# Keeping GpSimd's indirect transfers apart in a pooled-attention and top-1 mixture-of-experts kernel

## The chip, the cores and the metric

The kernel runs on one core of one Trainium2 chip. The metric is device time in microseconds (us) for one execution, the median of several runs; lower is better. The core's engines are named as in the profile: PE (TensorE, matmul), PEld (its weight loads), DVE (VectorE), ACT (ScalarE), POOL (GpSimd) and SP (SyncE, which here only issues DMAs).

## The reference

q, k and v are of shape 8 x 8 x 1152 x 64 (batch, heads, sequence, head size). Queries are averaged in pairs, attention is taken over the 576 pooled queries, and its output, one row of 512 per pooled query, goes through a mixture of 8 experts of which each token uses the one with the largest logit:

```python
q_pool = q.reshape(B, H, S // 2, 2, D).mean(axis=3)
attn = softmax(q_pool @ k.T / sqrt(D)); x = (attn @ v) as 4608 rows of 512
expert_idx = argmax(x @ w_gate); gate_w = softmax(x @ w_gate) at expert_idx
for e in range(8):                      # w1[e]: 512 x 1024, w2[e]: 1024 x 512
    out[mask_e] = gate_w[mask_e] * (relu(x[mask_e] @ w1[e]) @ w2[e])
```

## The kernel before, in words

**Attention** goes over 8 batches, 4 pairs of heads each, two halves of the queries per pair. PE makes the scores (`scores`, L521: 9 steps of 8 matmul records per half), DVE scales them and takes the minimum (L525), a small matmul and a reduce make one bias for the half (L543, L549), ACT takes the exponent (L553), POOL folds the chunks for the sums (L599) and PE multiplies with v (`values`, L624). For the last three pairs of the last batch PE makes the sums from the unfolded chunks (L594), and POOL has no folds.

**Routing** (`routing`) follows each batch: logits, the expert of each token, its place in that expert's list. ACT, DVE and SP write the batch's rows to a DRAM buffer `x_runs` (`put`), and POOL writes token numbers and weights into the experts' lists with six indirect scatters of 96 entries (`enlist`, L799). For batches 0 to 5 their keys spread them over the next batch's work; for the last two all six have one key.

**Experts.** After batch 6 two early slots of 384 tokens are chosen (`first_slots`); their tokens come by 24 indirect gathers (`gather`, L899, 32 tokens of four runs each per gather) while batch 7 is computed. Batch 7's rows and list entries wait for all 24 (`hold`). Then come eight experts by rank, with slots of 384+288, 384+256, 384+224, 384+192, 384+160, 224+192, 352 and 160 tokens: 14 slots, 3968 tokens, 124 gathers. `tokens_of` loads a list's piece (L883), makes indices (L893, L896) and gathers; `turn_tokens` weighs (L1056, L1057), turns (L1060) and splits the tokens in two parts (L1064, L1019); `first_products` (L1113) and `second_products` (L1141) multiply in three passes; ACT copies y out (L1153), and POOL scatters each block of up to 128 rows to `out` (L1148), 41 scatters in all.

**The order.** Nothing is scheduled by the compiler. Each piece of work is a step of a `Flow` with an engine, an assumed duration, a key, its predecessors and the buffers it holds. `Flow.emit` simulates the engines with these durations, taking on each engine the ready step of smallest key, and so makes one order of all steps; `Flow.trace` writes the instructions out in that order. Each engine then runs its own instructions in that order, held back only by data and buffers. The assumed durations that matter here: a score or value step 460 ns on PE; a first-product step `6 * n / 2.4 + 13` ns (16 of them for a slot of n tokens); a second-product step `6 * DM / 2.4 + 14` = 1294 ns (4 for each block of 128 rows); on POOL a gather 1310, an output scatter 1300, a list scatter 1230 ns. The order does not keep POOL from running ahead of PE on the chip.

The framework adds the waits for data. Two indirect writes into one DRAM tensor are made to wait for each other unless they are declared independent, which `enlist` does for `lists` and nothing does for `out`.

Of the kernel before, what the change touches and what calls it, by code (L numbers as in the profile page):

```python
# [62 lines left out]
FILL = 3  # L63
WARM = 2
SWITCH = 150

LATE = dict(PE=200, DVE=130, ACT=130, POOL=60, SP=100, DMA=1700, DMA2=1700)
OWN = dict(PE=0, DVE=200, ACT=220, POOL=100, SP=0, DMA=0, DMA2=0)
# [20 lines left out]
class Flow:  # L89


    def __init__(self, room=None, old=(), new=(), swap=None):

        self.room, self.steps = room, []
        self.old, self.new, self.swap = set(old), set(new), swap

    def add(self, eng, ns, fn, key=0.0, after=(), holds=(), tiled=False, late=0):
# [5 lines left out]
        step = [key, len(self.steps), eng, ns, fn, list(holds), 0, [], True, list(after), tiled, late]  # L103
# [6 lines left out]
    def carry(self, eng, ns, fn, key, after, holds, move, late=0):  # L110

        s = self.add(eng, ns, fn, key, after, holds)
        return s and self.add("DMA2" if eng == "POOL" else "DMA", move, lambda: None, key, [s], holds, late=late + (1200 if eng == "POOL" else 0))

    def emit(self):
# [12 lines left out]
        tiled, blocked = False, {}  # L128
        order, waiting = [], [s for s in self.steps if self.uses(s, self.old)]

        def unheld():
# [98 lines left out]
    def trace(self, order):  # L230

        todo = sum(self.uses(s, self.old) for s in order)
        while order:
# [5 lines left out]
            for s in order:  # L239
# [13 lines left out]
def kernel(  # L253
# [250 lines left out]
    def scores(o, f, key, x, half, step=None):  # L504
# [8 lines left out]
        for c in range(NC):  # L513
            pt = hold_of("st", lambda h: o.ps_s.tile([P, 2, 512], F32, **h.own("st")))

            def product(c=c, pt=pt):

                for i in range(2):
                    for h in range(2):
                        up, to = slice(h * D, (h + 1) * D), slice(i * D, (i + 1) * D)  # L520
                        nc.tensor.matmul(pt.t[to, h, :HQ], x.kT.t[up, c * P + i * D:c * P + (i + 1) * D], x.qT.t[up, cols],  # L521
                                         start=True, stop=True, tile_position=(up.start, to.start))

            def take(c=c, pt=pt):
                nc.vector.tensor_scalar(  # L525
# [87 lines left out]
    def values(o, f, key, x, s, ready, hp, half, xT):  # L613
# [4 lines left out]
        for c in range(NC):  # L618
            def product(c=c):

                for i in range(2):
                    for h in range(2):
                        up, cs = slice(i * D, (i + 1) * D), slice(h * D, (h + 1) * D)
                        nc.tensor.matmul(pa.t[cs, i, :HQ], x.vn.t[up, h, c, :], s.t[up, c, h],  # L624
                                         start=c == 0, stop=c == NC - 1, tile_position=(up.start, cs.start))

            p = f.add("PE", 460, product, key + 20.0 * c / NC, done(p, x.v, ready[c]), [pa, x.vn, s], QUADS)
        a = f.add("ACT", act(HQ) - 44, lambda: nc.scalar.copy(xT.t[:, hp, to], pa.t[:, 0, :HQ]), key + 20, done(p), [pa, xT])
# [38 lines left out]
    stores = []  # L667

    def routing(o, f, key, b, xT, rec, sums, ready, hold=()):

# [127 lines left out]
        def enlist(j):  # L798
# [4 lines left out]
            if b is not None:  # L803

                for other in stores:
                    tc.declare_no_dep(ins.ins, other.ins, reason="places in the lists are unique")
                stores.append(ins)

        outs = [c]
        for g in range(NB):  # L810
            outs.append(put(g))
        for j in range(NJ):
            outs.append(f.carry("POOL", 1230, lambda j=j: enlist(j), at + (K_PUT if b is None or b < B - 2 else 0) * j / NJ, done(p, *hold), [di, re], 40))
        return outs

    def first_slots(o, f, key, ready):
# [46 lines left out]
    def tokens_of(o, f, key, tab, s, n, known, stored, early=False, m=None):  # L863
# [43 lines left out]
        x.rows = done(*(f.carry("POOL", 1310, lambda i=i: gather(i), key + i * 3 / x.nb, done(p, *stored), [x.ix, x.xr[i // NQD]], 400)  # L907
                        for i in range(x.nb)))
        return x

# [182 lines left out]
    def first_products(o, m, f, x, key):  # L1093
# [6 lines left out]
        for f0 in range(0, NFC, nb):  # L1100
# [5 lines left out]
            for i in range(nb):  # L1106
                for c0 in range(0, NDC, 2):
                    def product(i=i, c0=c0, f0=f0, view=view):
                        (wh, wl), (xh, xl) = x.w1[(f0 + i) // 2].t, x.x.t
                        fp = slice((f0 + i) % 2 * P, (f0 + i) % 2 * P + P)  # L1110
                        for c in (c0, c0 + 1):
                            for k, (a, b) in enumerate(((wh, xh), (wh, xl), (wl, xh))):
                                nc.tensor.matmul(view()[:, i, :], a[:, c, fp], b[:, c, :n],  # L1113
                                                 start=c == 0 and k == 0, stop=c == NDC - 1 and k == 2)

                    p = f.add("PE", 6 * n / 2.4 + 13, product, at,
                              done(p, *x.w1_ready[(f0 + i) // 2], *x.turned),
# [9 lines left out]
    def second_products(o, m, f, x, key):  # L1127

        for r in range(x.nr):
# [5 lines left out]
            for c0 in range(0, NFC, 2):  # L1135
                def product(r=r, c0=c0, py=py):
                    (wh, wl), (hh, hl) = x.w2[c0 // 2].t, hidden(m)
                    hs = slice(r * P, (r + 1) * P)
                    for c in (c0, c0 + 1):
                        for k, (a, b) in enumerate(((hh, wh), (hh, wl), (hl, wh))):  # L1140
                            nc.tensor.matmul(py.t, a[:, c, hs], b[:, c % 2, :],  # L1141
                                             start=c == 0 and k == 0, stop=c == NFC - 1 and k == 2)

                p = f.add("PE", 6 * DM / 2.4 + 14, product, at + c0, done(p, *x.w2_ready[c0 // 2], *x.made.get(c0, ()), *x.made.get(c0 + 1, ())),
                          [py, x.w2[c0 // 2], *x.h[c0:c0 + 2]])

            def scatter(r=r, y=y, up=up):
                nc.gpsimd.indirect_dma_start(  # L1148
                    out=out, out_offset=bass.IndirectOffsetOnAxis(ap=x.re.t[:up, r:r + 1], axis=0),
                    in_=y.t[:up], in_offset=None, bounds_check=NT - 1, oob_is_err=False,  # L1150
                )

            a = f.add("ACT", act(DM) + 50, lambda y=y, py=py, up=up: nc.scalar.copy(y.t[:up], py.t[:up]),  # L1153
                      at, done(p), [py, y])
            f.carry("POOL", 1300, scatter, at, done(a), [y, x.re], 1200)


    with ExitStack() as cm, ExitStack() as units, ExitStack() as pairs:
        o, m = open_attention(False, cm, pairs, units), Pools()

        def swap_units():
            units.close()
            add_moe(m, units, "tile", side="right")

        f = Flow(dict(bank=BANKS, st=S_BUFS, s=UNITS, kn=1, qn=1, vn=3, kp=1, qp=1, kT=KT_BUFS, qT=KT_BUFS,
                      fold=FOLD_BUFS, sums=1, pa=1, sm=1, xT=2, rec=2, row=ROW_BUFS, lw=1, ex=1, de=1,
                      ohb=1, di=2, re=2, rec2=RE_BUFS, li=LI_BUFS, ix=LI_BUFS, xr=XR, xq=XR2, xt=XT, raw=RAW, x=1, **{f"{w}{j}": 1 for w in ("w1", "w2") for j in range(4)}, **{f"h{c}": 1 for c in range(NFC)}, ph=2, py=2, y=Y_BUFS),
                 ("kT", "qT", "vn", "fold", "s", "st"), ("x", "xt", "xq", *(f"{w}{j}" for w in ("w1", "w2") for j in range(4)), *(f"h{c}" for c in range(NFC)), "ph", "py", "y"), swap_units)
        hold = []
        pw = bank(o)  # L1170

# [115 lines left out]
```

## Time and profile before

| | |
|---|---|
| time, median of 3 runs | 1312.04 us (1309.75 to 1315.79) |
| the profiled execution: time, span | 1304.89 us, 1303.3 us |
| mean granted PE clock | 0.967 |
| busy: PE, DVE, ACT, POOL | 1222.0, 771.5, 637.5, 862.1 us |
| attention, to the first matmul of an expert | 0 to 790 us |
| experts | 790 to 1292 us |

A row of a timeline gives start and duration in us, engine, line, operation, output and inputs, how many instructions were merged, and in brackets how long the engine had been idle and what released it. A busy PE is no PE at its peak: a matmul's end is modelled, and at half clock it is busy for longer. The clock column PEclk is the clock that was granted, 1.00 being 2.4 GHz and 0.50 being 1.2 GHz.

### The profile page before, as it was taken

What the parts mean: (1) busy time and instruction counts of PE and PEld (TensorE: products, weight loads), DVE (VectorE), ACT (ScalarE), POOL (GpSimd) and SP (SyncE); (2) the same over time, 40 slices, a digit from 0 to 9 for tenths busy, and PEclk for the clock granted to TensorE, in tenths of its full rate; (3) what the DMA queues carried; (4) which work ended last, traced back from release to release, by engine and by line L of the source; (5) the groups of instructions that cost most, each with busy time, mean ns of one, the idle gap of its engine ahead of it and who ended that gap; (6) DMA issues with size and microseconds to landing.
All of it is one profiled execution on the core that took longest, in us unless ns stands there. A gap on an engine that the chain in (4) does not pass through costs nothing. (4 is left out here: it accounts for less than half of the span.)

```text
span 1303.3 us, 32720 instructions
## 1 busy us (share of the span) xinstructions
PE 1222.0 (94%) x13677; PEld 844.5 (65%) x13677; DVE 771.5 (59%) x2080; ACT 637.5 (49%) x832; POOL 862.1 (66%) x539
## 2 busy tenths in 40 slices
PE   7999999999999999999999598898689889999995
PEld 3555555555555555555555157797578779899895
DVE  5777777767767768768776067663334435425440
ACT  4666666656666666666574046332223323424440
POOL 2999799798998998998992701577475755300110
PEclk8999999999999999999999699999798899999998
DMA  5523233323333333323324205652333434414330
GB/s 165 140 82 93 87 93 94 95 74 105 98 92 110 78 93 104 85 89 98 91 77 152 50 2 140 211 167 57 108 109 96 124 91 128 128 69 146 104 100 19
DMA packets 73517, 131.75 MB, mean 101 GB/s; under 512 B 9347, under 2 KB 32799, under 8 KB 73360
## 3 DMA queue, kind: packets, MB, share of 16 engines
q1 hardware_dynamic: 62528, 109.89, 28.8%
q0 software_dynamic: 9744, 19.64, 5.4%
q8 instruction: 110, 1.80, 0.7%
q14 instruction: 47, 0.39, 0.1%
q10 hardware_dynamic: 1088, 0.03, 0.1%
HBM read 108.75 MB, written 21.02 MB: 100 GB/s over the span
## 5 line engine op out<-in xcount | busy, mean ns | idle before, releaser
L525 DVE TENSOR_SCALAR_CACHE_REDUCE s<-st 128x576 f32<-128x576 f32 x576 | 424.5, 754 | 166.9 <-PE st L521 162.6
L553 ACT ACTIVATE s<-s,bias 128x1728 f32<-128x1728 f32 x192 | 325.3, 1733 | 172.5 <-DVE bias L549 168.2
L521 PE MATMUL st<-qT,kT 64*64 64x288 f32 x4608 | 374.8, 413 | 10.1 <-DVE bias L549 4.9
L624 PE MATMUL pa<-s,vn 64*64 64x288 f32 x4608 | 357.8, 405 | 3.6 <-issue 3.5
L521 PEld LDWEIGHTS st<-qT,kT 64*64 64x64 f32 x4608 | 160.5, 133 | 135.4 <-DVE s L525 30.0
L624 PEld LDWEIGHTS pa<-s,vn 64*64 64x64 f32 x4608 | 171.8, 133 | 102.9 <-issue 9.5
L599 POOL TENSOR_TENSOR fold<-s 128x1728 f32<-128x1728 f32 x58 | 224.3, 3875 | 14.3 <-ACT s L553 9.3
L599 POOL TENSOR_TENSOR fold<-fold,s 128x1728 f32<-128x1728 f32 x58 | 224.1, 3873 | 1.1
L1113 PE MATMUL ph<-xh,w1h 128*128 128x384 f32 (+6 forms) x512 | 162.9, 318 | 31.7 <-DVE hl L1121 22.0
L1113 PE MATMUL ph<-xl,w1h 128*128 128x384 f32 (+6 forms) x512 | 161.2, 315 | 0.7 <-DVE xl L1019 0.6
L1113 PE MATMUL ph<-xh,w1l 128*128 128x384 f32 (+6 forms) x512 | 160.8, 314 | 0.0
L1148 POOL DMA_INDIRECT out_dram<-y,rec x41 | 44.0, 1072 | 174.2 <-ACT y L1153 158.3
L899 POOL DMA_INDIRECT xr<-x_runs,ix x104 | 111.4, 1072 | 65.7 <-issue 26.8
L1121 DVE SCALAR_TENSOR_TENSOR hl<-ph,hh 128x384 fp32r<-128x384 f32 (+5 forms) x100 | 54.8, 550 | 148.3 <-ACT hh L1119 114.0
L1119 ACT ACTIVATE hh<-ph 128x384 fp32r<-128x384 f32 (+5 forms) x100 | 48.8, 488 | 187.4 <-PE ph L1113 139.6
L1141 PE MATMUL py<-w2h,hh 128*128 128x512 f32 x328 | 129.4, 394 | 4.0 <-issue 4.0
L1141 PE MATMUL py<-w2l,hh 128*128 128x512 f32 x328 | 129.0, 393 | 0.0
L1141 PE MATMUL py<-w2h,hl 128*128 128x512 f32 x328 | 128.9, 393 | 0.0
L1113 PEld LDWEIGHTS ph<-xh,w1h 128*128 128x128 f32 x512 | 100.8, 197 | 37.0 <-DVE hl L1121 25.0
L799 POOL DMA_INDIRECT lists<-re,di x48 | 44.7, 932 | 99.0 <-DVE di L759 65.7
L1113 PEld LDWEIGHTS ph<-xl,w1h 128*128 128x128 f32 x512 | 101.0, 197 | 1.9 <-DVE xl L1019 0.9
L1113 PEld LDWEIGHTS ph<-xh,w1l 128*128 128x128 f32 x512 | 100.9, 197 | 0.0
(176 smaller groups left out, 1372.6 us busy)
## 6 DMA issues: line engine op xcount, KB each, us to landing
raw<-in_moe_w_dram SPq DMA_DIRECT2D x80, 512.0 KB
kn<-in_k_dram SPq DMA_DIRECT2D x32, 576.0 KB
qn<-in_q_dram SPq DMA_DIRECT2D x32, 576.0 KB
vn<-in_v_dram SPq DMA_DIRECT2D x32, 576.0 KB
x_runs<-row SPq DMA_DIRECT2D x24, 396.0 KB
xr<-x_runs,ix POOLq DMA_INDIRECT x104
x_runs<-empty SPq DMA_DIRECT2D x4, 297.0 KB
lists<-re,di POOLq DMA_INDIRECT x48
```

The costliest lines, as they stand in the source:

```text
L521: nc.tensor.matmul(pt.t[to, h, :HQ], x.kT.t[up, c * P + i * D:c * P + (i + 1) * D], x.qT.t[up, cols], start=True, stop=True, tile_position ...
L525: nc.vector.tensor_scalar(s.t[:, c], pt.t[:, :, :HQ], -SCALE, None, op0=ALU.mult, op1=ALU.min, accum_out=mx.t[:, c:c + 1],)
L553: nc.scalar.activation(s.t[:, c0:c0 + n], s.t[:, c0:c0 + n], AF.Exp, bias=bias.t, scale=-1.0)
L599: add = lambda to, a, b: nc.gpsimd.tensor_tensor(to, a, b, ALU.add)
L624: nc.tensor.matmul(pa.t[cs, i, :HQ], x.vn.t[up, h, c, :], s.t[up, c, h], start=c == 0, stop=c == NC - 1, tile_position=(up.start, cs.start))
L799: ins = nc.gpsimd.indirect_dma_start(out=lists, out_offset=bass.IndirectOffsetOnAxis(ap=di.t[:, j:j + 1], axis=0), in_=re.t[:, j, :], in_o ...
L899: nc.gpsimd.indirect_dma_start(out=x.xr[i // NQD].t[:, i % NQD, :], out_offset=None, in_=xg, in_offset=bass.IndirectOffsetOnAxis(ap=x.ix.t ...
L1113: nc.tensor.matmul(view()[:, i, :], a[:, c, fp], b[:, c, :n], start=c == 0 and k == 0, stop=c == NDC - 1 and k == 2)
L1119: a = f.add("ACT", act(nb * n) - 44, lambda fs=fs, view=view: nc.scalar.activation(hidden(m)[0][:, fs, :n], view(), AF.Relu), at - 20, don ...
L1121: d = f.add("DVE", dve(nb * n), lambda fs=fs, view=view: nc.vector.scalar_tensor_tensor(hidden(m)[1][:, fs, :n], view(), 0.0, hidden(m)[0] ...
L1141: nc.tensor.matmul(py.t, a[:, c, hs], b[:, c % 2, :], start=c == 0 and k == 0, stop=c == NFC - 1 and k == 2)
L1148: nc.gpsimd.indirect_dma_start(out=out, out_offset=bass.IndirectOffsetOnAxis(ap=x.re.t[:up, r:r + 1], axis=0), in_=y.t[:up], in_offset=Non ...
```

## The change

Three things. (1) The steps of the list scatters, the gathers and the output scatters are marked `paced`. In `emit`, after a paced step no other paced step may start on POOL until its assumed end plus `CALM` = 1300 ns; other POOL steps may. (2) In `trace`, each paced instruction is given a wait for the PE instruction that was last written out before it, so that it starts no sooner than that one has ended. For this the product functions return their last matmul. (3) Output scatters are declared independent of each other. The core of the diff:

```diff
+CALM = 1300
 class Flow:
-    def __init__(self, room=None, old=(), new=(), swap=None):
+    def __init__(self, room=None, old=(), new=(), swap=None, pace=None):
         self.room, self.steps = room, []
+        self.pace, self.pe = pace, None
...
@@ emit
                     if other is not None and s[0] > other[0] + KEEP:
                         skipped.append(s)
                         break
+                    if s[12] and now < calm:
+                        skipped.append(s)
+                        continue
...
                 free[e] = start + s[3]
+                if s[12]:
+                    calm = free[e] + CALM
+                    heapq.heappush(events, (calm, -1, 2, s))
...
@@ trace
-                s[4]()
+                made = s[4]()
+                if s[2] == "PE" and hasattr(made, "ins"):
+                    self.pe = made
+                if s[12] and self.pe is not None:
+                    self.pace(made, self.pe)
...
@@ routing, tokens_of: the carry of enlist and of gather
+            ..., paced=True
...
@@ second_products
             def scatter(r=r, y=y, up=up):
-                nc.gpsimd.indirect_dma_start(
+                ins = nc.gpsimd.indirect_dma_start(
...
+                if f.room is not None:
+                    for other in written:
+                        tc.declare_no_dep(ins.ins, other.ins, reason="a token stands in one list once")
+                    written.append(ins)
+                return ins
...
-            f.carry("POOL", 1300, scatter, at, done(a), [y, x.re], 1200)
+            f.carry("POOL", 1300, scatter, at, done(a), [y, x.re], 1200, paced=True)
...
+        def in_step(ins, pe):
+            tc.add_manual_dep(ins.ins, pe.ins.name, mybir.DependencyInfo(
+                mybir.DependencyClass.Sync, mybir.DependencyReason.DATA), reason="no sooner than its place in the order")
```

## Rows read from the trace of the kernel before

**Rows 1.** The page's first part: busy us (share of the span) and instructions.

```profile
PE 1222.0 (94%) x13677; PEld 844.5 (65%) x13677; DVE 771.5 (59%) x2080; ACT 637.5 (49%) x832; POOL 862.1 (66%) x539
```

**Rows 2.** Busy time by stretches of 50 us: the stretch, its length, busy us (instructions) of each engine, granted PE clock, DMA share, GB/s.

```profile
700.00:750.00 50.00, 34.73 (x358) 15.58 (x354) 14.10 (x47) 7.01 (x9) 24.00 (x24) 0.79 0.35 100
...
900.00:950.00 50.00, 37.41 (x188) 32.70 (x187) 16.94 (x29) 12.82 (x21) 28.31 (x33) 0.86 0.33 96
...
1100.00:1150.00 50.00, 50.00 (x287) 45.27 (x287) 22.12 (x34) 18.20 (x28) 14.32 (x14) 1.00 0.38 120
```

**Rows 3.** Timeline of POOL: the first and the last of batch 6's six list scatters, and of the 24 early gathers.

```profile
688.78 0.92 POOL L799 DMA_INDIRECT lists<-re,di  x1 [3.64 <-DVE top L546]
...
694.89 0.92 POOL L799 DMA_INDIRECT lists<-re,di  x1 [0.30 <-issue]
715.36 1.06 POOL L899 DMA_INDIRECT xr<-x_runs,ix  x1 [19.54 <-DMA raw<-in_moe_w_dram]
...
745.36 1.00 POOL L899 DMA_INDIRECT xr<-x_runs,ix  x1 [0.30 <-issue]
```

**Rows 4.** Timeline of PE beside these two runs of transfers.

```profile
692.95 0.70 PE L594 MATMUL sums<-s,ones 128*32 128x288 f32 x4 [0.45 <-issue]
...
697.24 0.79 PE L594 MATMUL sums<-s,ones 128*32 128x288 f32 x8 [0.79 <-issue]
...
715.98 5.77 PE L594 MATMUL sums<-s,ones 128*32 128x288 f32 x58
722.46 0.71 PE L594 MATMUL sums<-s,ones 128*32 128x288 f32 x4 [0.71 <-issue]
...
729.62 0.37 PE L543 MATMUL st<-ident,top 64*64 64x64 f32 x2 [1.08 <-issue]
...
749.74 1.24 PE L521 MATMUL st<-qT,kT 64*64 64x288 f32 x8 [4.93 <-DVE bias L549]
```

**Rows 5.** Timeline of DVE at the end of the early gathers.

```profile
749.39 0.29 DVE L549 TENSOR_REDUCE bias<-st 128x1 f32<-128x128 f32 x1 [30.62 <-remote]
```

**Rows 6.** Three stretches, columns as in Rows 2: the early gathers, just behind them, and behind a stall of PE among the experts.

```profile
716.00:749.00 33.00, 18.46 (x100) 5.76 (x96) 2.66 (x10) 0.03 (x1) 23.36 (x24) 0.70 0.23 52
749.00:754.00 5.00, 4.26 (x44) 2.36 (x48) 2.74 (x9) 4.22 (x3) 0.00 (x0) 0.60 0.00 0
...
846.00:852.00 6.00, 6.00 (x19) 6.00 (x20) 2.88 (x6) 1.42 (x2) 4.78 (x5) 0.50 0.52 139
```

**Rows 7.** Timelines of POOL and DVE in batch 0's list scatters: the third of three in a row, DVE's wait beside it, and a lone one with DVE behind it.

```profile
142.87 0.92 POOL L799 DMA_INDIRECT lists<-re,di  x1 [0.30 <-issue]
...
143.85 0.76 DVE L525 TENSOR_SCALAR_CACHE_REDUCE s<-st 128x576 f32<-128x576 f32 x1 [2.16 <-PE st L521]
...
148.65 0.92 POOL L799 DMA_INDIRECT lists<-re,di  x1
...
148.89 0.76 DVE L525 TENSOR_SCALAR_CACHE_REDUCE s<-st 128x576 f32<-128x576 f32 x1 [0.33 <-PE st L521]
```

**Rows 8.** The page's costliest groups and the same by form: line, engine, operation, count, busy us, mean ns, idle before and its releasers.

```profile
L899 POOL DMA_INDIRECT xr<-x_runs,ix x104 | 111.4, 1072 | 65.7 <-issue 26.8
...
L799 POOL DMA_INDIRECT lists<-re,di x48 | 44.7, 932 | 99.0 <-DVE di L759 65.7
...
L1060 DVE STREAM_TRANSPOSE xt<-xr 128x512 f32<-128x512 f32 x25 | 17.3, 699 | 0.0
```

**Rows 9.** Timelines of PE and ACT: the second matmul of the first early slot; the copies of y that end the second early slot, the slot before a 384 slot, that 384 slot, and the last slot.

```profile
791.09 0.69 PE L1113 MATMUL ph<-xl,w1h 128*128 128x384 f32 x1 [0.60 <-DVE xl L1019]
...
870.35 0.59 ACT L1153 COPY y<-py 128x512 f32<-128x512 f32 x1 [0.31 <-PE py L1141]
...
1084.33 0.59 ACT L1153 COPY y<-py 96x512 f32<-96x512 f32 x1 [0.35 <-PE py L1141]
...
1117.46 0.59 ACT L1153 COPY y<-py 128x512 f32<-128x512 f32 x1 [4.85 <-PE py L1141]
...
1290.32 0.57 ACT L1153 COPY y<-py 32x512 f32<-32x512 f32 x1 [4.85 <-PE py L1141]
```

**Rows 10.** Timelines of POOL, DVE, PE and ACT among the experts: a gather, DVE's wait for its data, PE's wait behind it; and a late ACT in a longer run of gathers.

```profile
841.87 1.01 POOL L899 DMA_INDIRECT xr<-x_runs,ix  x1 [0.30 <-issue]
...
844.57 0.17 DVE L1056 TENSOR_TENSOR xr<-xr,li 128x16 f32<-128x16 f32 x1 [7.08 <-DMA xr<-x_runs,ix]
...
845.99 0.69 PE L1113 MATMUL ph<-xh,w1h 128*128 128x384 f32 x1 [4.14 <-DVE xr L1057]
...
927.19 0.41 ACT L1119 ACTIVATE hh<-ph 128x288 fp32r<-128x288 f32 x1 [9.32 <-remote]
```

**Rows 11.** From the chain that ended last (start, duration, what) the scatter before the last; from POOL's timeline the last scatter.

```profile
1285.75 4.63 DMA out_dram<-y,rec
...
1291.17 0.87 POOL L1148 DMA_INDIRECT out_dram<-y,rec  x1 [4.44 <-ACTq L1226]
```

**Rows 12.** DMA queues (kind: packets, MB, share of 16 engines) in 722 to 748 us, where this is the only queue with packets: none of the instruction queues has one.

```profile
q0 software_dynamic: 640, 1.35, 23.3%
```

**Rows 13.** Timeline of POOL: batch 7's first list scatter, the first load of a list's piece, the first gather of a ranked slot.

```profile
807.74 0.95 POOL L799 DMA_INDIRECT lists<-re,di  x1 [61.38 <-DVE di L759]
...
824.14 0.79 POOL L883 DMA_DIRECT2D li<-lists  x1 [4.54 <-DVE t_took L927]
...
835.47 2.08 POOL L899 DMA_INDIRECT xr<-x_runs,ix  x1 [0.28 <-POOL rec L896]
```

More of the change, by code (lines that the diff above doesn't have):

```diff
@@ L89, with add @@
 class Flow:
-    def __init__(self, room=None, old=(), new=(), swap=None):
+    def __init__(self, room=None, old=(), new=(), swap=None, pace=None):
         self.room, self.steps = room, []
+        self.pace, self.pe = pace, None
         self.old, self.new, self.swap = set(old), set(new), swap
-    def add(self, eng, ns, fn, key=0.0, after=(), holds=(), tiled=False, late=0):
+    def add(self, eng, ns, fn, key=0.0, after=(), holds=(), tiled=False, late=0, paced=False):
         if self.room is None:
@@ L102, in add @@
             h.left += 1
-        step = [key, len(self.steps), eng, ns, fn, list(holds), 0, [], True, list(after), tiled, late]
+        step = [key, len(self.steps), eng, ns, fn, list(holds), 0, [], True, list(after), tiled, late, paced]
         for a in after:
@@ L108, in add, with carry @@
         return step
-    def carry(self, eng, ns, fn, key, after, holds, move, late=0):
-        s = self.add(eng, ns, fn, key, after, holds)
+    def carry(self, eng, ns, fn, key, after, holds, move, late=0, paced=False):
+        s = self.add(eng, ns, fn, key, after, holds, paced=paced)
         return s and self.add("DMA2" if eng == "POOL" else "DMA", move, lambda: None, key, [s], holds, late=late + (1200 if eng == "POOL" else 0))
@@ L127, in emit @@
             users[s[2]] += self.uses(s, self.old)
-        tiled, blocked = False, {}
+        tiled, blocked, calm = False, {}, 0.0
         order, waiting = [], [s for s in self.steps if self.uses(s, self.old)]
@@ L520, in product @@
                         up, to = slice(h * D, (h + 1) * D), slice(i * D, (i + 1) * D)
-                        nc.tensor.matmul(pt.t[to, h, :HQ], x.kT.t[up, c * P + i * D:c * P + (i + 1) * D], x.qT.t[up, cols],
+                        made = nc.tensor.matmul(pt.t[to, h, :HQ], x.kT.t[up, c * P + i * D:c * P + (i + 1) * D], x.qT.t[up, cols],
                                          start=True, stop=True, tile_position=(up.start, to.start))
+                return made
             def take(c=c, pt=pt):
@@ L623, in product @@
                         up, cs = slice(i * D, (i + 1) * D), slice(h * D, (h + 1) * D)
-                        nc.tensor.matmul(pa.t[cs, i, :HQ], x.vn.t[up, h, c, :], s.t[up, c, h],
+                        made = nc.tensor.matmul(pa.t[cs, i, :HQ], x.vn.t[up, h, c, :], s.t[up, c, h],
                                          start=c == 0, stop=c == NC - 1, tile_position=(up.start, cs.start))
+                return made
             p = f.add("PE", 460, product, key + 20.0 * c / NC, done(p, x.v, ready[c]), [pa, x.vn, s], QUADS)
@@ L665, in attend @@
         return done(*outs)
-    stores = []
+    stores, written = [], []
     def routing(o, f, key, b, xT, rec, sums, ready, hold=()):
@@ L812, in routing @@
         for j in range(NJ):
-            outs.append(f.carry("POOL", 1230, lambda j=j: enlist(j), at + (K_PUT if b is None or b < B - 2 else 0) * j / NJ, done(p, *hold), [di, re], 40))
+            outs.append(f.carry("POOL", 1230, lambda j=j: enlist(j), at + (K_PUT if b is None or b < B - 2 else 0) * j / NJ, done(p, *hold), [di, re], 40, paced=True))
         return outs
@@ L898, in gather @@
         def gather(i):
-            nc.gpsimd.indirect_dma_start(
+            return nc.gpsimd.indirect_dma_start(
                 out=x.xr[i // NQD].t[:, i % NQD, :], out_offset=None, in_=xg,
@@ L906, in tokens_of @@
         p = f.add("DVE" if early else "POOL", 650, index, key - LEAD, done(p), [x.li, x.ix, x.re])
-        x.rows = done(*(f.carry("POOL", 1310, lambda i=i: gather(i), key + i * 3 / x.nb, done(p, *stored), [x.ix, x.xr[i // NQD]], 400)
+        x.rows = done(*(f.carry("POOL", 1310, lambda i=i: gather(i), key + i * 3 / x.nb, done(p, *stored), [x.ix, x.xr[i // NQD]], 400, paced=True)
                         for i in range(x.nb)))
@@ L1112, in product @@
                             for k, (a, b) in enumerate(((wh, xh), (wh, xl), (wl, xh))):
-                                nc.tensor.matmul(view()[:, i, :], a[:, c, fp], b[:, c, :n],
+                                made = nc.tensor.matmul(view()[:, i, :], a[:, c, fp], b[:, c, :n],
                                                  start=c == 0 and k == 0, stop=c == NDC - 1 and k == 2)
+                        return made
                     p = f.add("PE", 6 * n / 2.4 + 13, product, at,
@@ L1140, in product @@
                         for k, (a, b) in enumerate(((hh, wh), (hh, wl), (hl, wh))):
-                            nc.tensor.matmul(py.t, a[:, c, hs], b[:, c % 2, :],
+                            made = nc.tensor.matmul(py.t, a[:, c, hs], b[:, c % 2, :],
                                              start=c == 0 and k == 0, stop=c == NFC - 1 and k == 2)
+                    return made
                 p = f.add("PE", 6 * DM / 2.4 + 14, product, at + c0, done(p, *x.w2_ready[c0 // 2], *x.made.get(c0, ()), *x.made.get(c0 + 1, ())),
@@ L1147, in scatter @@
             def scatter(r=r, y=y, up=up):
-                nc.gpsimd.indirect_dma_start(
+                ins = nc.gpsimd.indirect_dma_start(
                     out=out, out_offset=bass.IndirectOffsetOnAxis(ap=x.re.t[:up, r:r + 1], axis=0),
@@ L1151, in scatter @@
                 )
+                if f.room is not None:
+                    for other in written:
+                        tc.declare_no_dep(ins.ins, other.ins, reason="a token stands in one list once")
+                    written.append(ins)
+                return ins
             a = f.add("ACT", act(DM) + 50, lambda y=y, py=py, up=up: nc.scalar.copy(y.t[:up], py.t[:up]),
                       at, done(p), [py, y])
-            f.carry("POOL", 1300, scatter, at, done(a), [y, x.re], 1200)
+            f.carry("POOL", 1300, scatter, at, done(a), [y, x.re], 1200, paced=True)
     with ExitStack() as cm, ExitStack() as units, ExitStack() as pairs:
@@ L1167 @@
                       ohb=1, di=2, re=2, rec2=RE_BUFS, li=LI_BUFS, ix=LI_BUFS, xr=XR, xq=XR2, xt=XT, raw=RAW, x=1, **{f"{w}{j}": 1 for w in ("w1", "w2") for j in range(4)}, **{f"h{c}": 1 for c in range(NFC)}, ph=2, py=2, y=Y_BUFS),
-                 ("kT", "qT", "vn", "fold", "s", "st"), ("x", "xt", "xq", *(f"{w}{j}" for w in ("w1", "w2") for j in range(4)), *(f"h{c}" for c in range(NFC)), "ph", "py", "y"), swap_units)
+                 ("kT", "qT", "vn", "fold", "s", "st"), ("x", "xt", "xq", *(f"{w}{j}" for w in ("w1", "w2") for j in range(4)), *(f"h{c}" for c in range(NFC)), "ph", "py", "y"), swap_units, in_step)
         hold = []
```

## The prediction

> **What bounds the kernel now.** The page's first part shows PE busy for 94% of the span [rows 1], so I read the stretches of 50 us first, to find where PE is not at full rate [rows 2]. Two places stand out: 700 to 750, with 34.7 us of PE and a clock of 0.79, and the experts' first half (37.4 us at 0.86 in 900 to 950). From 1100 on PE is full.
>
> In 700 to 750 the timelines of POOL and PE, laid side by side, show what happens. POOL issues 24 gathers back to back, one per 1.30 us [rows 3]. PE runs at full rate until 715.98 + 5.77 = 721.75, then gets 2 to 4 matmuls per 1.4 us, with idle time for which the trace has no releaser, until 749.74 [rows 4]. DVE's bias waits 30.6 us for a matmul that ended at 730, and goes on 3 us after the last gather [rows 5]. Batch 6's six list scatters, one per 1.22 us, do the same in small: PE stutters from about 692.5 to 697.95 [rows 3, 4]. So signals between engines come late while a run of indirect transfers lasts. A run of three held DVE for up to 2.2 us, a lone one for 0.3 [rows 7]: the run's length matters.
>
> Among the experts there are two kinds of stall. In runs of gathers ACT sees a finished product up to 9 us late; and DVE, which takes its work in order, stands 7.1 us at a weighing whose gather has not landed, so that PE waits 4.1 us behind it [rows 10]. After such a stop PE works at 1.2 GHz for some 6 us [rows 6], which costs 3 more. In sum: a slot of 384 takes 1117.46 - 1084.33 = 33.1 us at full rate [rows 9], and the planner assumes 16 x 973 + 12 x 1294 ns = 31.1, a ratio of 1.065. The 14 ranked slots are 343 us by the planner, so 365 at the chip's rate; from 870 to the last copy at 1290.3 they took 420 [rows 9], 55 too many. The two early slots lost another 7. So 62 us of waiting and low clock.
>
> The tail offers nothing: the scatter before the last lands at 1290.38, before y is copied (1290.32 + 0.57), and the last scatter starts at 1291.17 [rows 9, 11].
>
> **The change part by part.** *Runs broken up.* Between 721.75 and 749.74 PE did matmuls worth about 2.5 us (14 sums at 5.77 / 58 us each, 24 others at half that); 25.5 of the 28 were lost, and 2 more to the low clock behind them [rows 4, 6]. The six list scatters cost 5.4 less 1.6 of work, 3.9. Bounds: nothing comes back (each transfer holds the engines by itself) or all 31.4 does. I take all of it, since a lone transfer shows no hold [rows 7].
>
> *POOL's pace.* A paced step now takes 1.31 + 1.30 = 2.61 us of the plan, for 1.30 on the chip before. I work in the trace's own times, since what is won in attention moves all that follows.
>
> First the early gathers. In the plan 24 gathers last 24 x 2.61 = 62.6 us, and up to 66.7 at the ratio of 1.065 found above; I take 66; the list scatters before them, now apart, start them some 4 us later: they land near 719 + 66 = 785. Batch 7's list scatters wait for all of them; those started at 807.7 [rows 13], and would now be due 31.4 earlier, at 776: 9 us late. They then take six times 2.7 instead of 1.22, 9 longer, but the lists' load stood until 824.1 for DVE, some 7 us behind the lists [rows 13]. So the first ranked gather comes 11 later against PE: at 846.5 for 835.5.
>
> Then the ranked slots. PE is free for them in the plan at about 858 (791.1, two slots of 31.1, 5 for logits and low clock). A slot's tokens are ready at 846.5 + 2.61 per paced step up to its last gather + 5.1 (planned landing, weighing, turning, splitting). The output scatters of slots two back come before a slot's gathers by their keys, so these are steps 14, 40, 66, 90 and 113 for the five 384 slots and 151 for the 352. With 58.3, 51.9, 50.6, 49.3 and 48.0 + 37.7 us of planned PE work in between, PE waits there for 30, 9.5, 16, 12, 11 and 13.5 us in the plan, 92 in all.
>
> On the chip it is less. While PE has nothing to do, no product is written out and the gathers have no new wait, so they follow at 1.30 us. Of each planned wait 7.7 us are the last gather's way to PE and the rest gathers at 2.61: (92 - 6 x 7.7) / 2.61 = 17 gathers, 17 x 1.30 = 22. The way itself is 844.57 - 841.87 = 2.7 us to DVE [rows 10], then four passes of 0.7 [rows 8] and hand-offs, 6.0. Waits 6 x 6 + 22 = 58, clock 6 x 3 = 18: 76 or 77, for 62 before. **+15.** Bounds: the six latencies alone (36 + 18 = 54, so -8) and the planned waits unshortened (92 x 1.065 + 18 = 116, so +54).
>
> *Each wait for a product.* Behind a waiting transfer on POOL stand folds in attention and index work or further gathers later. It costs POOL at most one product step, 0.46 x 1.065 = 0.49 us in attention, for 36 list scatters of batches 0 to 5 at most 18 us, against 99 us in which POOL already stood idle before list scatters [rows 8], some 30 of them in attention, and four buffers between the folds and PE. I take 2, between 0 and 18. Its other side is that POOL, once late, can catch up at 1.30.
>
> *Scatters not waiting for each other.* At the tail nothing (above); among the experts the 2.7 us that a scatter takes to land are mostly covered by POOL's wait for y, and POOL is not what ends there once gathers wait for PE. Nothing.
>
> Sum: -31.4 + 15 + 2 = -14. From the profiled execution's 1304.9 this gives 1290.5; that execution lies 7 below the median of the runs, so from the median 1312 - 14 = **1298 us**.
>
> **A rule against the trace.** DVE waits 30.6 us beside gathers [rows 5], while the only queue with packets is POOL's own [rows 12]. The Trainium skill, SBUF — State Buffer, section "SBUF: two separate sides", says that GpSimd and VectorE share a pair of ports as an exclusive lock for a whole instruction, and that PE never waits on anyone. By that rule each transfer would hold DVE for its own length wherever it stands, and spacing would win nothing: the first rival. The trace speaks against it, since PE, which holds no such lock, stops as well, and a lone transfer holds nobody.
>
> **The rivals.** *The hold belongs to each transfer, not to the run* (slower). Then 24 gathers hold PE for 24 x 1.15 us wherever they are put, attention wins nothing, and POOL's pace costs its 15 + 2: 1312 + 17 = 1329. For it: PE's stutter has about the period of a transfer [rows 4]. Against: rows 7. It decides once less than 10 of the 31.4 come back. Chance 0.12.
>
> *The gathers set the pace and do not catch up* (slower). If their waits sit behind products that themselves wait, the planned 92 us stand at the chip's rate: -31.4 + 54 + 2, 1336. For it: 2.61 us a step is more than PE needs (15 steps, 39 us, per 384 slot of 33.1). Against: nothing is written out while PE starves. Chance 0.10; it decides when the experts lose over 100 us.
>
> *POOL keeps ahead after all* (faster by far). If the output scatters stand behind the gathers, their 34 x 2.61 us fall out of the way, and only the first ranked slot and two or three others wait: some 40 us instead of 77, so -14 - 37 = -51, 1261. For it: before, the gathers were some three slots ahead by 1100, limited by buffers. Chance 0.20.
>
> *The change does not do what it says*: POOL is behind its order on the chip, each product has long ended, and transfers still follow at 1.30. Then 1312, give or take 4. For it: the first ranked gathers came late [rows 10]. Against: in the early gathers POOL was otherwise idle. Chance 0.10.
>
> **How the numbers follow.** My forecast has 0.48, with a range of its own from 1283 to 1311 (12 us to either side for the count of waits and the chain behind the early gathers). About 0.5%, 6.6 us, is what a measurement here can tell from no change: below 1305.4 is faster, above 1318.6 slower. Faster: 0.37 of the forecast, 0.20 of the third rival, 0.02 elsewhere, 0.59. Slower: 0.11 and 0.10 of the first two and 0.02, 0.23. Same: 0.18. The range for 8 in 10 goes from 1258, at the third rival, to 1330, at the first.
>
> **What would show it.** In the profile after, the early gathers stand 2 to 3 us apart over some 65 us; DVE's 30.6 us wait and PE's stutter are gone, and the first expert matmul comes near 760. PE's waits among the experts are then for gathers (DVE on xr and xq), at the head of the larger slots, 6 to 17 us each, and ACT's late starts of 4 to 9 us without a releaser are gone. The first ranked gather comes near 815. The last two scatters look as before. The prediction is wrong if PE still stutters beside gathers 2.6 us apart, if PE does not wait at the larger slots, or if POOL's folds fall behind in attention.

## The result and the profile after

The changed kernel took 1329.15 us (median of 4 runs, 1326.92 to 1333.14) beside 1310.89 us for the kernel before: a ratio of 1.0144, with a 95% interval of 1.011 to 1.0177. It is 18 us slower where 14 faster were forecast. The profiled execution has a span of 1327.2 us.

The page's first part, and three stretches of 50 us that answer to [rows 1, 2]:

```profile
PE 1211.8 (91%) x13677; PEld 841.8 (63%) x13677; DVE 778.4 (59%) x2080; ACT 637.0 (48%) x832; POOL 875.9 (66%) x539
```

```profile
700.00:750.00 50.00, 50.00 (x779) 28.52 (x771) 33.79 (x115) 23.44 (x22) 13.80 (x14) 1.00 0.34 99
...
900.00:950.00 50.00, 42.18 (x220) 36.79 (x219) 21.78 (x35) 16.21 (x26) 23.90 (x25) 0.93 0.43 128
...
1100.00:1150.00 50.00, 40.08 (x219) 34.90 (x219) 21.48 (x32) 14.95 (x21) 21.85 (x24) 0.88 0.40 118
```

The stretch that was to be mended is mended: PE is busy in all of 700 to 750 (34.7 us before). But 1100 to 1150, which was full, has lost 10 us. POOL's timeline shows the early gathers over 56 us where before they took 30 [rows 3]. The first 14 stand mostly 2 to 5 us apart; the last ten, from 764.08 on, follow one another without a wait:

```profile
724.29 1.06 POOL L914 DMA_INDIRECT xr<-x_runs,ix  x1 [14.72 <-DVE ix L908]
728.86 1.02 POOL L914 DMA_INDIRECT xr<-x_runs,ix  x1 [3.51 <-PE st L533]
731.29 1.01 POOL L914 DMA_INDIRECT xr<-x_runs,ix  x1 [1.40 <-PE pa L637]
...
779.96 1.42 POOL L914 DMA_INDIRECT xr<-x_runs,ix  x1 [0.30 <-issue]
```

PE's timeline has the first expert product and, behind it, every wait of over 5 us among the experts:

```profile
769.36 0.44 PE L1128 MATMUL ph<-xh,w1h 128*128 128x384 f32 x1 [4.62 <-ACT xh L1079]
...
868.55 0.69 PE L1128 MATMUL ph<-xh,w1h 128*128 128x384 f32 x1 [27.91 <-ACT xh L1079]
...
1010.70 0.69 PE L1128 MATMUL ph<-xh,w1h 128*128 128x384 f32 x1 [11.08 <-ACT xh L1079]
...
1079.05 0.69 PE L1128 MATMUL ph<-xh,w1h 128*128 128x384 f32 x1 [10.96 <-ACT xh L1079]
...
1146.24 0.69 PE L1128 MATMUL ph<-xh,w1h 128*128 128x384 f32 x1 [9.88 <-ACT xh L1079]
...
1257.93 0.66 PE L1128 MATMUL ph<-xh,w1h 128*128 128x352 f32 x1 [10.67 <-ACT xh L1079]
```

Five stops at the heads of the large slots, 70.5 us in sum, all for tokens (`xh`, the turned and split rows). ACT's copies of y that end the early slots and the last slot, against [rows 9]:

```profile
840.67 0.59 ACT L1175 COPY y<-py 128x512 f32<-128x512 f32 x1 [0.30 <-PE py L1157]
...
1313.36 0.57 ACT L1175 COPY y<-py 32x512 f32<-32x512 f32 x1 [4.85 <-PE py L1157]
```

So the early slots end 29.7 us earlier than before (870.35), and the 14 ranked slots take 472.7 us for 420.0. That is the whole result of these two executions: 30 won, 53 lost (1328.85 us against 1304.89; by the medians 18 are lost).

How one stop is made is seen at 1000, in the timelines of POOL, DVE and ACT; PE had stopped at 999.6:

```profile
999.89 1.03 POOL L914 DMA_INDIRECT xr<-x_runs,ix  x1 [1.14 <-PE py L1157]
...
1002.54 1.26 POOL L914 DMA_INDIRECT xr<-x_runs,ix  x1 [0.30 <-issue]
...
1005.45 1.00 POOL L1165 DMA_INDIRECT out_dram<-y,rec  x1 [0.31 <-issue]
...
1008.35 0.18 DVE L1071 TENSOR_TENSOR xr<-xr,li 128x16 f32<-128x16 f32 x1 [4.82 <-DMA xr<-x_runs,ix]
...
1010.03 0.62 ACT L1079 CAST xh<-xt 128x512 fp32r<-128x512 f32 x1 [7.56 <-DVE xt L1075]
```

Three gathers of the slot were still to be issued when PE ran dry. They follow at 1.3 us, with nothing left to wait for; the data is at DVE 5.8 us after the last one's start, and PE goes on 2.4 later. Of POOL's idle time before its gathers, the page's groups put the largest shares down to products of PE; before the output scatters the largest share has no releaser (issue).

```profile
L914 POOL DMA_INDIRECT xr<-x_runs,ix x104 | 118.1, 1136 | 132.0 <-PE ph L1128 43.0
L1165 POOL DMA_INDIRECT out_dram<-y,rec x41 | 44.3, 1081 | 121.5 <-issue 43.6
L914 POOL DMA_INDIRECT xq<-x_runs,ix x44 | 52.8, 1201 | 63.7 <-PE py L1157 43.0
```

### The profile page after: what moved, and what is told of

Its sections match the earlier page's. It is cut to its first block, busy times and chain, and to the rows that moved or that the text cites. A ratio compares the mean times of both kernels' runs of the same rounds, so it can differ in the third digit from the quotient of the medians.

```text
span 1327.2 us, 32820 instructions
## 1 busy us (share of the span) xinstructions
PE 1211.8 (91%) x13677; PEld 841.8 (63%) x13677; DVE 778.4 (59%) x2080; ACT 637.0 (48%) x832; POOL 875.9 (66%) x539
## 5 line engine op out<-in xcount | busy, mean ns | idle before, releaser
L533 PE MATMUL st<-qT,kT 64*64 64x288 f32 x4608 | 367.6, 412 | 4.6 <-DVE s L538 4.2
L637 PE MATMUL pa<-s,vn 64*64 64x288 f32 x4608 | 353.7, 407 | 3.1 <-DVE xT L643 2.4
L914 POOL DMA_INDIRECT xr<-x_runs,ix x104 | 118.1, 1136 | 132.0 <-PE ph L1128 43.0
L914 POOL DMA_INDIRECT xq<-x_runs,ix x44 | 52.8, 1201 | 63.7 <-PE py L1157 43.0
```

Source lines behind the costliest of these rows:

```text
L533: made = nc.tensor.matmul(pt.t[to, h, :HQ], x.kT.t[up, c * P + i * D:c * P + (i + 1) * D], x.qT.t[up, cols], start=True, stop=True, tile_p ...
L637: made = nc.tensor.matmul(pa.t[cs, i, :HQ], x.vn.t[up, h, c, :], s.t[up, c, h], start=c == 0, stop=c == NC - 1, tile_position=(up.start, c ...
L914: return nc.gpsimd.indirect_dma_start(out=x.xr[i // NQD].t[:, i % NQD, :], out_offset=None, in_=xg, in_offset=bass.IndirectOffsetOnAxis(ap ...
```

## The experiments

Kernels of one group (one letter; h1 and h2 are two) ran on one chip, beside the kernel before. In the first group the kernel before took 1245 us, not 1311; that became the second question. The table reads each kernel's timelines: the start of the first expert product, then from there to the copy of y that ends the second early slot, and from there to the last copy. "Order" is the time without a product among the experts in the kernel's own order, by the durations that `emit` assumes.

| kernel | time / before | first product | early slots | ranked slots | order |
|---|---|---|---|---|---|
| before, first profile | 1311 | 790.0 | 80.3 | 420.0 | 0.8 |
| after, first profile | 1329 / 1311 | 769.4 | 71.3 | 472.7 | 82.9 |
| f2, before again | 1247 | 753.1 | 79.9 | 399.1 | 0.8 |
| f1, after again | 1326 / 1248 | 766.3 | 71.1 | 474.2 | 82.9 |
| e1, pace without waits | 1295 / 1245 | 762.3 | 72.4 | 448.9 | 82.9 |
| e2, waits without pace | 1261 / 1245 | 757.9 | 82.5 | 409.5 | 0.8 |
| e3, lists and early gathers alone | 1259 / 1245 | 767.0 | 73.9 | 403.2 | 9.4 |
| e4, output scatters free | 1271 / 1245 | 765.1 | 72.0 | 418.4 | 26.5 |
| f3, CALM 600 | 1269 / 1248 | 768.4 | 82.3 | 401.9 | 7.4 |
| f4, early gathers alone | 1253 / 1248 | 753.7 | 82.4 | 402.4 | 0.8 |
| h1, the same, CALM 600 | 1247 / 1247 | 752.5 | 80.2 | 400.4 | 0.8 |
| h2, as h1 | 1285 / 1310 | 766.2 | 83.7 | 420.8 | 0.8 |

**The order or the waits (e1, e2).** From the changed kernel:

```diff
# e1
-                if s[12] and self.pe is not None:
-                    self.pace(made, self.pe)
# e2
-CALM = 1300
+CALM = 0
```

> The changed kernel without the waits for products; its order, with the paced steps 2.61 us apart, and the independent scatters stay. Theory A (the order starves PE: the kernel's own order, by its assumed durations, already has 83 us without a product among the experts, and output scatters between the gathers keep POOL from running ahead): the stalls of PE at the heads of the large slots stay, some 60 to 80 us of idle time, and the early gathers follow back to back again and hold PE for 27 us, so 1335 to 1360. Theory B (the waits bind POOL to a slow order, and without them it would run ahead as in the kernel before): the stalls go, the early hold comes back, 1305 to 1318.

> The changed kernel with CALM = 0: the order of the kernel before, each indirect transfer still waiting for the product ahead of it. Theory A: the order has under 1 us without a product among the experts, so the stalls of 10 us and more go; the early gathers stand 1.31 us apart in the order, about 1.4 on the chip, so most of the early hold stays: 1295 to 1320. Theory B (waits bind): stalls stay in some measure, 1325 or more. Theory C (a hold belongs to each transfer, wherever it stands): about as the kernel before, 1312.

e1 took 1295.14 (ratio to before 1.0396, 1.0371 to 1.0421), e2 1261.17 (1.0118, 1.009 to 1.0146). Both times lie under what theory A gave, as does e3's below, because the kernel before was itself 66 us faster there. By the ranked slots, against f2 (another chip, with the kernel before within 3 us), the order alone costs 50 us, the waits alone 10, both together 75 (f1). PE's stops stand at the same slots without any wait for a product (e1's timeline):

```profile
861.60 0.69 PE L1126 MATMUL ph<-xh,w1h 128*128 128x384 f32 x1 [26.93 <-ACT xh L1077]
...
992.61 0.69 PE L1126 MATMUL ph<-xh,w1h 128*128 128x384 f32 x1 [6.17 <-ACT xh L1077]
```

So theory A holds for the larger part: the order starves PE. The waits deepen each later stop, from 6 us to 11 (f1). Theory B falls for this part: without the waits the stops stand, and POOL does not get ahead of PE. e1 showed something else too. Its 24 early gathers stand back to back, and in this execution PE does not notice (POOL's timeline, then stretches of 6 us):

```profile
718.08 1.06 POOL L912 DMA_INDIRECT xr<-x_runs,ix  x1 [20.30 <-DMA raw<-in_moe_w_dram]
...
748.52 1.00 POOL L912 DMA_INDIRECT xr<-x_runs,ix  x1 [0.30 <-issue]
```

```profile
722.00:728.00 6.00, 6.00 (x104) 3.77 (x100) 4.33 (x12) 0.34 (x1) 4.70 (x5) 1.00 0.26 58
...
734.00:740.00 6.00, 6.00 (x104) 3.79 (x100) 4.72 (x12) 4.99 (x3) 4.66 (x5) 1.00 0.26 59
```

**Which transfers (e3, e4).**

```diff
# e3: lists and early gathers alone          e4: the last pair of lines alone
-    ..., [x.ix, x.xr[i // NQD]], 400, paced=True)
+    ..., [x.ix, x.xr[i // NQD]], 400, paced=early)
-    f.carry("POOL", 1300, scatter, at, done(a), [y, x.re], 1200, paced=True)
+    f.carry("POOL", 1300, scatter, at, done(a), [y, x.re], 1200)
```

> Pace and waits kept for list scatters and the 24 early gathers alone; ranked gathers and output scatters as in the kernel before, except that they stay independent. Theory A and B: the 30 us won before the experts stay, one stall of about 8 us that the order has at the first ranked slot is added, and the ranked slots lose what they lost before: 1282 to 1296. Theory C: no gain, 1312.

> As the changed kernel, but output scatters are neither paced nor made to wait; lists and all gathers are. Theory A: the order keeps 26 us of the 83 us without a product, nearly all at the first ranked slot, and its end comes 56 us earlier; the holds by runs of gathers stay away: 1265 to 1285. Theory B (each gather's wait for a product is what costs): about as the changed kernel, 1320 to 1330. Theory C: 1312 and more.

e3 took 1259.29 (1.0109, 1.0083 to 1.0136), e4 1271.33 (1.0205, 1.018 to 1.0231). Freeing the 41 output scatters takes 56 us from the ranked slots (474.2 to 418.4), which is what it takes from the order (82.9 to 26.5). e4 frees them of the pace and of the waits together; no run parts the two. It keeps one large stop, the first, as its order has it:

```profile
865.29 0.69 PE L1128 MATMUL ph<-xh,w1h 128*128 128x384 f32 x1 [28.29 <-ACT xh L1079]
```

**The same kernels again, and two smaller doses (f1 to f4).** f1 and f2 are the changed kernel and the kernel before, unchanged. f3 and f4:

```diff
# f3
-CALM = 1300
+CALM = 600
# f4: early gathers alone, as e3, and the lists free
-    f.carry("POOL", 1230, lambda j=j: enlist(j), ..., [di, re], 40, paced=True)
+    f.carry("POOL", 1230, lambda j=j: enlist(j), ..., [di, re], 40)
```

> The changed kernel as it is, beside the kernel before on one chip. In the first four experiments the kernel before took 1245 on its chip, and 24 gathers in a row (in the changed kernel without waits) left PE at full rate there. Theory A (the order starves PE, whatever the chip; a hold by runs of transfers is there on some chips only): five stalls of 9 to 28 us at the heads of the same slots as in the first profile, together 70 us, on either kind of chip; 1315 to 1330, while the kernel before takes about 1245 on a chip without holds and about 1311 on one with them. Theory C (the chip is faster in everything): after would fall by the same 5% as before did, to 1262.

> The kernel before, for its profile on this chip. If it takes about 1245: PE at full rate beside the 24 gathers at 1.30 us (50 us of PE in 700 to 750 where the first profile had 34.7), no wait of DVE of 30 us there, and in the ranked slots ACT's late starts of 4 to 9 us without a releaser gone, some 35 us less from the second early slot to the end. If it takes about 1311: all as in the first profile.

> The changed kernel with CALM = 600, so 1.91 us for a paced step of the order in place of 2.61. By its assumed durations the order has 7 us without a product among the experts, all at the first ranked slot, and ends 73 us earlier than with 1300. Theory A: one stall of 10 to 15 us is left, 1250 to 1268 on either kind of chip (holds may come back in part where transfers now stand 1.9 apart: up to 20 more on a chip with holds). Theory B (the waits for products cost, not the pace): 1300 or more.

> Pace and waits for the 24 early gathers alone; all else in the order of the kernel before, scatters of outputs independent. The order has under 1 us without a product among the experts, and its early gathers stand from 714.7 to 774.8. On a chip without holds: 1245 to 1255, since there is nothing to win, and batch 7's lists wait for the early gathers (7 us later in the order). On a chip with holds: 27 us won before the experts, 1280 to 1292.

The changed kernel took 1326.45 beside 1248.22 (1.063, 1.0612 to 1.0648), with its stops at the same slots and of the same length (f1's timeline):

```profile
864.78 0.69 PE L1128 MATMUL ph<-xh,w1h 128*128 128x384 f32 x1 [27.37 <-ACT xh L1079]
...
1007.11 0.69 PE L1128 MATMUL ph<-xh,w1h 128*128 128x384 f32 x1 [10.97 <-ACT xh L1079]
```

f2 is the kernel before without holds (a hold: PE, DVE or ACT standing still beside indirect transfers, with nothing in the trace that explains it). Its gathers are as tight as in [rows 3], and PE is at full rate beside them, where [rows 6] have 18.46 of 33 (POOL's timeline, then the stretch of 33 us that these gathers fill):

```profile
707.30 1.06 POOL L899 DMA_INDIRECT xr<-x_runs,ix  x1 [14.99 <-DVE ix L893]
...
737.39 1.38 POOL L899 DMA_INDIRECT xr<-x_runs,ix  x1 [0.30 <-issue]
```

```profile
707.00:740.00 33.00, 32.84 (x535) 18.47 (x528) 22.41 (x69) 13.98 (x11) 24.47 (x24) 1.00 0.40 121
```

Nor does any of ACT's `hh` start late without a releaser, as in [rows 10]. By these two executions holds cost the kernel before 37 us up to the first product, nothing in the early slots and 21 in the ranked ones (790.0, 80.3, 420.0 against 753.1, 79.9, 399.1; for the ranked slots some 35 were expected). Without holds the change costs 78 us.

The changed kernel takes 1326 in this group and took 1329 in the first measurements, where the kernel before met holds. That its pace kept them away there is not shown by this: its first trace has no sign of a hold at all, not even beside its last ten early gathers, which stand close. There PE is as busy as in f1 (11.96 of 12 us; the stretch of the first trace):

```profile
770.00:782.00 12.00, 11.91 (x70) 10.93 (x71) 10.18 (x21) 9.45 (x23) 9.55 (x7) 0.86 0.81 254
```

So its executions may have met none. The trace that bears on it is h2's, below.

f3 took 1268.80 (1.0175, 1.0151 to 1.0198), just above the 1250 to 1268 of theory A: the ranked slots are within 3 us of f2, but attention lasts 15 longer. f4 took 1252.87 (1.0038, 1.0022 to 1.0054). Between e3 and f4 stands the pace of the list scatters, and it costs attention 13 us (767.0 against 753.7).

**Scatters alone, and the early gathers once more (g1, g2).** g1 is the kernel before with part (3) of the change and nothing else; g2 is f4 again.

> The kernel before with nothing but the independent output scatters. Theory A and the prediction: no difference that can be measured, within 3 us of the kernel before on its chip, since POOL's wait for y covers the landing of the scatter ahead. A rival (POOL is kept from its gathers by scatters that wait for the one ahead): 5 to 15 us faster.

> Pace and waits for the 24 early gathers alone, on a further chip. If the kernel before takes about 1311 here (a chip with holds): 1280 to 1292, and PE at full rate from 715 to 750, which is the 27 us that the prediction counts for the early gathers. If it takes about 1246: 3 to 6 us slower than before, as in the last group.

g1: 1246.54 beside 1246.81, 1.0001 (0.9992 to 1.001). Nothing, as forecast. g2: 1254.04 (1.0062, 1.0047 to 1.0078), 7 us slower than before where 3 to 6 were expected; no holds in this group either.

**A version meant to keep the gain (h1, h2, i1, i2).** h1, h2 and i2 are f4 with CALM = 600; i1 is f3 again.

> Pace and waits for the 24 early gathers alone, and CALM = 600 in place of 1300. If the kernel before takes about 1246 on this chip: the order's early gathers end earlier than with 1300 and batch 7's lists wait for them less, so 0 to 4 us slower than before. If it takes about 1311 (a chip with holds): 1275 to 1300, since transfers 1.9 us apart may hold in part.

> The same kernel (pace and waits for the 24 early gathers alone, CALM = 600) on a further chip, to see whether the kernel before takes 1246 or 1311 there. If 1246: 1244 to 1252. If 1311, a chip with holds: 1275 to 1300.

> The changed kernel with CALM = 600 on a further chip. Theory A on a chip without holds (before 1246): 1267 to 1272, as in f3. On a chip with holds (before 1310): if spacing by 1.9 us keeps all holds away, the same 1267 to 1275, its ranked slots in 402 us; if holds among the ranked gathers come back, 1285 to 1295, ranked slots in 415 to 420.

> Pace and waits for the early gathers alone, CALM = 600. Chip without holds (before 1246): 1244 to 1250. Chip with holds (before 1310): 1280 to 1290, its ranked slots in 418 to 424 us, since they are as in the kernel before.

h1 took 1247.47 beside 1247.17 (0.9999, 0.9987 to 1.0012), i2 1245.84 beside 1247.87 (0.9991, 0.998 to 1.0001): no cost without holds. h2 met them: 1285.31 beside 1309.79, 24 us, one execution each. Its trace has both cases side by side: six list scatters in a row, with PE held (f2 has 10.00 of 10 us beside its six), then gathers in runs of up to three, with PE full (POOL's timeline, then stretches of 10 us):

```profile
689.55 0.92 POOL L813 DMA_INDIRECT lists<-re,di  x1 [3.67 <-DVE top L559]
...
695.66 0.92 POOL L813 DMA_INDIRECT lists<-re,di  x1 [0.30 <-issue]
718.97 1.06 POOL L914 DMA_INDIRECT xr<-x_runs,ix  x1 [22.40 <-DMA raw<-in_moe_w_dram]
...
725.04 1.00 POOL L914 DMA_INDIRECT xr<-x_runs,ix  x1 [2.39 <-PE st L533]
```

```profile
690.00:700.00 10.00, 6.90 (x77) 3.23 (x79) 4.84 (x34) 5.87 (x5) 5.05 (x6) 0.95 0.45 117
...
730.00:740.00 10.00, 9.96 (x155) 6.06 (x151) 6.57 (x19) 2.96 (x3) 4.97 (x5) 1.00 0.15 35
...
740.00:750.00 10.00, 9.93 (x157) 6.96 (x153) 6.28 (x19) 3.06 (x4) 4.99 (x6) 1.00 0.19 42
```

Its ranked slots, left as they were, took 420.8, as before. i1 (1268.76 beside 1247.87; 1.0212, 1.0149 to 1.0275) was to show whether 1.9 us apart also frees the ranked slots, but its traced execution, at 1266.66, met no holds, so that stays open (one of its four took 1283.14 and left no trace). The last group ran on the very chip of h2, so "a chip with holds", as the expectations have it, is wrong: one chip showed both.

## Why the prediction was wrong, point by point

**Runs broken up, -31.4: right in size; that the spacing did it rests on h2.** From batch 6's logits to the first expert product the kernel before took 790.05 - 676.34 = 113.7 us, the changed one 769.36 - 684.33 = 85.0 (PE's timelines, before and after):

```profile
676.34 1.18 PE L698 MATMUL sums<-xT,wg 128*32 128x288 f32 x16
```

```profile
684.33 1.18 PE L712 MATMUL sums<-xT,wg 128*32 128x288 f32 x16
```

That is 28.7 won, and 33.3 without the new 4.62 us wait at 769.36. f1, on a chip where the kernel before met no holds, takes 83.6 us for the same way. So the changed kernel ran as without holds; whether its spacing kept them away or it met none, this pair can't tell. For the spacing speaks h2, with 89.1 us (677.11 to 766.16) in an execution that had holds.

The rule of the Trainium skill that I set against the trace (SBUF — State Buffer, section "SBUF: two separate sides") I read too widely: there the lock on the ports that GpSimd and VectorE share makes a VectorE operation wait only in a 2-port mode or, against a GpSimd operation that reads SBUF, with two SBUF inputs, and `tensor_reduce` never contends on this chip. The DVE instruction that waited 30.6 us is such a reduce [rows 5], so the first rival does not follow from that rule. Nor does the rule explain the holds: in f2 DVE is busy for 22.41 of the 33 us beside gathers as tight as before, where it had 5.76 [rows 6].

**Each wait for a product, +2 (0 to 18): 8 in the first pair.** Batch 6's logits came 8.0 us later, and against f2 the first product 13 later (f1), with the pace alone 9 (e1) and with the waits alone 5 (e2). The step looked only at the waits; the pace that keeps list scatters 2.6 us apart in the order was not priced in attention at all. It costs 13 by e3 against f4, though PE's timeline in f1 shows only 6 us more of waiting than f2's from 100 to 685 us, and 3 more at the first expert product (4.62 against 1.49); where the rest lies was not found.

**POOL's pace, +15: this term failed, and with it the sign of the sum.** Among the experts (early and ranked slots) it was -9.0 + 52.7 = +43.7. Three parts of the step, by size:

- *The catch-up.* I counted 92 us of planned waits at six heads and let gathers at 1.30 us cut them to 58. The order itself has 78 at these heads (24.8, 5.5, 12.2, 12.2, 10.8, 12.8), and the chip took 72 (27.9, 1.7, 11.1, 11.0, 9.9, 10.7): next to nothing is caught up. At the usual head only three gathers were left when PE ran dry, and the way from the last one to PE is 8.2 us, not 6.0, since the landing, read as 2.7 us from one pair of [rows 10], took 5.8. At the first ranked slot POOL waited between its gathers for loads of lists and their indices, 20 us for ten gathers (POOL's timeline after, the first of them, an index and the last). This is 14 of the miss, and small waits of PE that I had not counted add 6 (78.3 us of waits in the ranked slots in all):

```profile
842.70 1.09 POOL L914 DMA_INDIRECT xr<-x_runs,ix  x1 [0.30 <-issue]
...
846.77 0.32 POOL L908 TENSOR_SCALAR ix<-li,gid 128x12 int32<-128x12 int32 x1 [0.88 <-DMA li<-lists]
...
863.14 1.37 POOL L914 DMA_INDIRECT xr<-x_runs,ix  x1 [0.30 <-issue]
```

- *The loss of before.* I took 365 us as the ranked slots' time at full rate, and so 55 as lost. But where PE does not wait, a slot of 160, of 192 or of 224 tokens takes the same 21.6 us (from the ends of the slots before them, 1117.46 [rows 9], 1172.10, 1193.70 and 1215.32). ACT's copies of y that end slots of 192, 160, 224 and 192 in the kernel before:

```profile
1139.07 0.58 ACT L1153 COPY y<-py 64x512 f32<-64x512 f32 x1 [0.35 <-PE py L1141]
...
1193.70 0.58 ACT L1153 COPY y<-py 32x512 f32<-32x512 f32 x1 [0.35 <-PE py L1141]
...
1215.32 0.58 ACT L1153 COPY y<-py 96x512 f32<-96x512 f32 x1 [4.89 <-PE py L1141]
...
1236.94 0.58 ACT L1153 COPY y<-py 64x512 f32<-64x512 f32 x1 [0.35 <-PE py L1141]
```

  The six small slots are 130 us, for the 116 of my ratio, and the full rate is an estimated 378. The loss of before was 42, so there was less to win: 13 of the miss.
- *The clock.* I counted 18 us for starts at 1.2 GHz. Six stretches of 5 to 7 us behind the stops have a granted clock of 0.50 to 0.57 and 29.7 us of PE in sum, about 14 lost, 4 less than counted. With 378 and 78 of waits this makes 470, against 472.7. The parts, 14, 6 and 13 less 4, make up the 29 by which the term was too small. Two of the six, columns as in [rows 2]:

```profile
868.00:873.00 5.00, 4.42 (x15) 4.02 (x15) 0.69 (x1) 0.65 (x2) 0.96 (x1) 0.57 0.11 31
...
1010.00:1015.00 5.00, 4.26 (x12) 3.86 (x13) 0.69 (x1) 1.10 (x2) 0.83 (x1) 0.50 0.00 0
```

**Scatters, 0: right** (g1). In e4 it was their pace and their waits, not their independence, that were worth 56 us.

**The rivals.** The measured 1329 is the number of the first rival (a hold by each transfer), but its mechanism fell: in h2, where six list scatters in a row held PE, gathers spread out did not, and in f2 and e1 24 gathers in a row held nobody. What happened is the second, the gathers setting the pace without catch-up (1336, given 0.10): with my own 365 the ranked slots lose 108 us, over its bound of 100 (95 with the 378 found above). The reason it gave, waits behind products that themselves wait, is at most a part: e1, without any such wait, still loses 50 us there. "Nothing is written out while PE starves" was true and did not help, since by then the late gathers were few. The third (POOL keeps ahead, since scatters fall out of the way) named the right lever, seen in e4, but not in this kernel. Of the signs, PE's full rate beside the early gathers, the end of ACT's late starts behind first products and the waits at the large slots came; the first expert product came at 769, not 760, and the first ranked gather at 831.69, not near 815 (behind lists that were 2.7 us apart and loads that waited for them until 824.61).

## What to carry to other kernels

When a planner's order gets a new spacing, first multiply it out against the engine that it feeds: between the third and the fourth large slot 24 steps of 2.61 us are 62.6, for 50.6 of PE's work, and the stops came 68.4 apart; of the 78 us that the order came up short at the large slots, 6 were caught up on the chip. Space only the run that does harm: the 24 early gathers alone, 1.9 us apart in the order, gave 24 us with holds (h2, one execution each) and cost nothing without (h1, i2). And before a stall is priced, see whether it is there in every execution: this one was worth some 60 us in two groups and nothing in five.

## What the runs showed of the hardware

- **Holds come and go.** The same kernel, with the same 1.30 us between gathers, took 1303 to 1316 us in the first measurements and 1310 beside h2, but 1242 to 1251 in the five other groups; the chip of h2 showed both. What decides it was not found; no experiment here could bring it about.
- **Length of the run.** Where holds are there (h2), six list scatters in a row left PE 6.9 us of 10, and gathers 1.9 us apart on average, at most three of them in a row, 9.9 to 10. But length alone does not decide: in the first profile of the kernel before, batch 7's six list scatters stand as close, one per 1.2 to 1.7 us from 807.74 on [rows 13], beside expert products, and PE is full there, with DVE at 8.3 of 9 us. What differs was not found (columns as in [rows 2]).

```profile
807.00:816.00 9.00, 9.00 (x50) 8.26 (x49) 8.29 (x25) 4.29 (x7) 6.00 (x6) 1.00 0.69 136
```

- **Small slots.** A slot of 160 tokens costs PE as much as one of 224, 21.6 us each in the kernel before.
